# Two layers of segmented memory attention and ReLU feed-forward: part of the first segment's elementwise work goes from VectorE to GpSimd

## The chip, the cores and the metric

The kernel runs on one core of a Trainium2 chip. The time is device microseconds of one execution. Five engines work side by side: TensorE (PE in the profile, PEld for its weight loads), VectorE (DVE), ScalarE (ACT), GpSimd (POOL) and SyncE (SP), which here only issues DMAs. Each engine has its own queue and takes its instructions strictly in order; they wait for each other through semaphores.

## What is computed

The input x has 2048 tokens of 640 features. Two layers follow each other with the same weights; each adds attention and then a feed-forward block to x, both on a layer-normalised x. Attention has 32 heads of 20 features and works in 4 segments of 512 tokens: causal softmax attention inside the segment, mixed by a gate per head with a read from a memory of the earlier segments.

```
phi = lambda t: jnp.where(t > 0, t + 1.0, jnp.exp(t))
g = _sigmoid(beta).reshape(1, H, 1, 1)
for s in range(N):
    qs, ks, vs = (q[:, :, s].copy(), k[:, :, s].copy(), v[:, :, s].copy())
    logits = jnp.einsum('bhqd,bhkd->bhqk', qs, ks) * scale + mask
    a_dot = jnp.einsum('bhqk,bhkd->bhqd', _softmax(logits, axis=-1), vs)
    pq = phi(qs)
    a_mem = num / den                    # pq @ M, pq @ z
    o = g * a_mem + (1.0 - g) * a_dot
    pk = phi(ks)
    M = M + jnp.einsum('bhld,bhle->bhde', pk, vs)
    z = z + jnp.einsum('bhld->bhd', pk)
x = x + o @ wo                           # then x = x + relu(ln(x) @ w1) @ w2
```

The kernel computes phi as min(exp(t), max(t, 0) + 1), which is the same function.

## The kernel before

Everything stays on the chip except the weights' and inputs' loading, a scratch copy of q and k in device memory, and the output.

**Order of the work.** Each engine's order is made when the program is built. Some thirty generators (scores, exps, causal, apply, divide, phi_, mem_write, ffn and so on) each yield one operation at a time: an engine or a choice of two, a planned duration, and what it waits for. A planner (Sched, L224) takes among the heads of all generators the one with the earliest planned start. Added to that start is an offset from the table SHIFT (L175), keyed by generator, phase and how far in the phase it is. A change of any planned duration or engine can give another order on every queue. `pool(600.0, ...)` is an operation of GpSimd planned at 600 ns; the numbers only steer the order.

**One segment of attention.** Normalised tokens (L831, or L843 for the first four tiles) are turned by DMA (L807), or by TensorE for the first four tiles (L856). TensorE projects q and k (L764 for whole weights, L767 for weights loaded in four quarters of 32 columns) and v; VectorE or ScalarE copies the result out of PSUM (L971 and L972 for q and k into stg, L1026 for v). q and k go to device memory and come back as pad, four heads on 32 partitions each (L1060, L1109; the first heads directly, L1089). Two groups of four heads make one step m of 10 half rounds: TensorE makes two halves at a time (one score round, L1293), ScalarE takes the exponential of each half (L1357, 128x1024), GpSimd zeroes what lies above the diagonal (L1369: 1, 2, 2, 1 and 2 selects in the five rounds of a step). TensorE then multiplies the probabilities by v (L1389; two groups of the first segment by tokens, L1428). The result is copied out (L1399, otu), turned by DMA (otk, L807), and divided by its row sum times 1 - g: a reciprocal (L1475), a product with omg (L1478), and two products of 128x320 (L1483, o_sb). The first segment has four steps: 40 exponentials, 32 selects, 20 score rounds; three of its steps go through L1483.

**Memory.** phi of the keys (L1136 max and add, L1138 exponential in place, L1139 min) is turned by DMA (phk), multiplied with v (L1230), copied to M_sb (L1245) and multiplied by maskg (L1257), which keeps each head's own block and carries the gate g. maskg is made once, in consts(): GpSimd fills it with ones (L711) and cuts the blocks out with ten selects (L716, L719); VectorE multiplies each of its five parts by g (L727). g and 1 - g come from L703 to L707. Later segments read the memory (L1172, L1184 to L1187) and add it (L1502).

**Afterwards** o_sb is turned (L807, oT), projected (L764 or L767 with wo_r), added to x (L1511), normalised (L785, L787, L797, rstd by a power on GpSimd, L801), and fed to the feed-forward block, whose last addition is L1606; results are stored by L1638 and L1634. Projections of later segments fill the time in which TensorE would wait for the exponentials of earlier ones.

The two helpers that choose the engine:

```
def dve(n, mode, fn, waits=(), extra=0.0, acq=None, urgent=False, port=False):
    op = Op([("dve", 66.0 + n / (0.96 * mode) + extra, [(fn, True)], 95.0)], waits, ...)
def pool(ns, fn, waits=()):
    return Op([("pool", ns, [(fn, True)], 60.0)], waits)
```

Of the kernel before, what the change touches and what calls it, by code (L numbers as in the profile page):

```python
# [12 lines left out]
DH = 20  # L13
# [146 lines left out]
class Spawn:  # L160
# [15 lines left out]
    (0, 0, 0): -12, (0, 1, 1): -26, (0, 2, 0): -50, (0, 3, 0): -50, (1, 0, 0): -312, (1, 0, 1): -1663,  # L176
    (1, 0, 2): -925, (1, 1, 0): 400, (1, 1, 2): -475, (1, 2, 0): 300, (1, 2, 2): 887, (1, 3, 1): 100, (1, 3, 2): 125,
    (1, 4, 2): 1000, (1, 5, 0): 700, (1, 5, 1): 675, (1, 5, 2): 700, (1, 6, 0): 575, (1, 6, 1): -500, (1, 6, 2): -288,
    (1, 7, 0): 100, (1, 7, 2): 300, (2, 0, 0): -100, (2, 0, 1): -663, (2, 0, 2): -1075, (2, 1, 0): 400,
    (2, 1, 1): -100, (2, 1, 2): -1175, (2, 2, 0): -275, (2, 2, 1): -275, (2, 2, 2): -275, (2, 3, 0): 2387,  # L180
    (2, 3, 2): 1125, (2, 4, 0): -700, (2, 4, 1): -7250, (2, 4, 2): 1951, (2, 5, 1): 388, (2, 5, 2): 725,
    (2, 6, 0): 2000, (2, 6, 1): 2237, (2, 6, 2): 2325, (2, 7, 0): -5250, (2, 7, 1): 2000, (2, 7, 2): 2000,
    (3, 0, 0): -288, (3, 0, 2): -575, (3, 2, 1): -188, (3, 3, 0): -75, (3, 3, 1): -50, (3, 5, 0): -50, (3, 6, 0): -50,
    (3, 6, 1): -250, (3, 7, 1): -350, (5, 0, 0): -5225, (5, 1, 0): 500, (5, 3, 0): -1988, (5, 5, 0): -100,
    (5, 6, 0): 50, (5, 7, 0): -3000, (6, 1, 1): -100, (6, 2, 0): 38, (6, 2, 1): 425, (6, 3, 0): 50, (6, 3, 1): -50,
    (6, 5, 0): 100, (6, 6, 1): -375, (7, 0, 0): -1500, (7, 1, 0): -1525, (7, 2, 0): -300, (7, 3, 0): 200,
    (7, 4, 0): -300, (7, 7, 0): -1500, (8, 2, 0): -774, (8, 2, 1): -75, (8, 2, 2): -6000, (8, 3, 1): -50,
    (8, 4, 0): -175, (8, 4, 1): -100, (8, 6, 0): -50, (8, 7, 0): 3000, (8, 7, 1): 3500, (8, 7, 2): 3000,
    (9, 0, 0): -25, (9, 0, 1): -88, (9, 0, 2): -100, (9, 2, 2): -1725, (9, 3, 0): -225, (9, 3, 1): -87,
    (9, 3, 2): -225, (9, 4, 1): -50, (9, 4, 2): -200, (9, 5, 0): -325, (9, 5, 1): -1388, (9, 5, 2): -200,  # L190
    (9, 6, 0): -400, (9, 6, 1): -287, (9, 6, 2): -1500, (9, 7, 0): 1000, (9, 7, 1): 1000, (9, 7, 2): 1000,
    (10, 0, 0): -100, (10, 0, 1): -37, (10, 1, 0): -1100, (10, 1, 1): -725, (10, 3, 0): 700, (10, 4, 1): -1500,
    (10, 5, 0): -100, (10, 5, 1): -600, (10, 6, 0): -1500, (10, 6, 1): 500, (10, 7, 1): -375, (11, 0, 0): -38,
    (11, 0, 1): -1276, (11, 1, 0): -1550, (11, 1, 1): -650, (11, 2, 0): -50, (11, 2, 1): -225, (11, 3, 0): -1075,
    (11, 3, 1): -3125, (11, 4, 1): 400, (11, 5, 1): -300, (11, 6, 0): -1000, (11, 6, 1): -50, (11, 7, 0): 700,
    (12, 0, 2): -225, (12, 1, 0): 2274, (12, 1, 1): 2274, (12, 2, 0): 5175, (12, 2, 1): -3537, (12, 3, 0): 125,
    (12, 3, 1): -700, (12, 4, 0): 3000, (12, 4, 1): 3000, (12, 5, 0): -375, (12, 5, 1): -200, (12, 6, 0): 4500,
    (12, 7, 0): 1500, (12, 7, 1): 4750, (13, 0, 0): -888, (13, 1, 0): 200, (13, 2, 0): 7413, (13, 3, 0): -50,
    (13, 4, 0): 300, (13, 5, 0): 2113, (13, 7, 0): 1100, (14, 1, 0): -225, (14, 2, 0): -300, (14, 3, 0): -1575,
    (14, 5, 0): -200, (14, 6, 0): -1000, (14, 7, 0): 7863, (15, 0, 0): -238, (15, 0, 1): -62, (15, 2, 0): -350,  # L200
    (15, 2, 1): -300, (15, 4, 1): 412, (15, 5, 0): 425, (15, 6, 1): -450, (16, 2, 1): 75, (16, 3, 0): 638,
    (16, 3, 1): -112, (16, 5, 0): 237, (16, 5, 1): 188, (16, 6, 0): 100, (16, 6, 1): 100, (16, 7, 0): -575,
    (16, 7, 1): -150, (17, 1, 0): 25, (17, 3, 0): -337, (17, 6, 1): -487, (17, 7, 1): 12, (18, 1, 1): -275,
    (18, 2, 1): -75, (18, 3, 0): -50, (18, 3, 1): -100, (18, 5, 1): 200, (19, 0, 0): 500, (19, 2, 0): 500,
    (19, 4, 0): 25, (19, 5, 0): -3850, (20, 1, 0): 138, (20, 1, 1): -75, (20, 2, 0): -200, (20, 2, 1): 50,
    (20, 4, 0): 63, (20, 4, 1): 225, (20, 5, 1): 25, (20, 6, 0): 50, (20, 6, 1): -700, (21, 0, 0): -1788,
    (21, 0, 1): 100, (22, 0, 0): 100, (23, 0, 0): -100, (26, 0, 0): 500, (27, 1, 0): -88, (27, 1, 1): -75,
    (27, 3, 1): 62, (27, 5, 0): 500, (27, 5, 1): 137, (27, 7, 0): 300, (27, 7, 1): 50, (28, 0, 0): 475,
# [287 lines left out]
def pool(ns, fn, waits=()):  # L496
    return Op([("pool", ns, [(fn, True)], 60.0)], waits)
# [8 lines left out]
def bass_interleave_layers__memory_aug_infini_attn__dense_activation_relu__prompt_kernel(  # L506
    nc, A_x, A_wq, A_wk, A_wv, A_wo, A_beta, B_x, B_w1, B_w2, out,
):
    with contextlib.ExitStack() as es:
# [169 lines left out]
        def consts():  # L679
# [6 lines left out]
                pattern=[[-1, 128]], channel_multiplier=1), [t0])  # L686
            S.set("ident", tks=[t1])
            th = yield pool(100, lambda e: e.memset(mhalf[:], -0.5))
            S.set("mhalf", tks=[th])
            yield Need("xt", 0, 0, 1)  # L690
            tv = []
            for b in range(2):
# [1044 lines left out]
```

## Time and profile before

| what | value |
|---|---|
| runs | 550.38, 552.99, 553.38 us; median 552.99 |
| the profiled execution | 550.77 us, of which span 548.3 us |
| TensorE clock granted | full in all of the span |
| first matmul's start, last matmul's end | 1.15 us, 545.4 us |
| first score round, 20th score round | 17.97 us, 58.21 us |
| first exponential, end of the 40th | 18.40 us, 60.58 us |
| busy 18 to 60 us, of 42: PE, DVE, ACT, POOL | 39.7, 39.6, 40.2, 26.7 us |
| busy 70 to 500 us, of 430: PE, DVE, ACT, POOL | 430.0, 352.0, 341.5, 160.5 us |
| DMA engines busy 18 to 36, 36 to 60, 70 to 500 us | 94%, 93%, 50% |

A row of the timeline has the start, the time from the first start to the last end of the merged instructions, engine, line, operation, out<-in, shape and count, and in brackets the idle time before it with what ended it. Neighbouring instructions of one engine overlap by about 0.08 us, so that a busy time is somewhat more than the pace. A busy TensorE is not TensorE at its pace, since the ends of matmuls are modelled; starts are measured.

### The profile page before, as it was taken

Reading aid. Unit: us, or ns where it says so; the run is one execution under the profiler, and the core shown is the slowest. Engines: PE = TensorE matmul, PEld = TensorE weight load, DVE = VectorE, ACT = ScalarE, POOL = GpSimd, SP = SyncE. Lnnn points to the kernel's source line nnn. Section 1 sums busy time; section 2 is a strip of 40 time slices with the busy share of each in tenths; the row PEclk is TensorE's granted clock in tenths of the full one; section 3 lists DMA queues with packets and bytes.
Section 4 is the critical chain, followed back from the end, with each engine's and each line's share of the span. In section 5 each row is a group of like instructions: output and inputs, shape, how many; then the busy total and the mean of one; then the engine's idle time right before and its main releaser. Section 6 shows DMA issues by size and latency. Waiting matters only on the chain.

```text
span 548.3 us, 22987 instructions
## 1 busy us (share of the span) xinstructions
PE 540.1 (99%) x10283; PEld 309.9 (57%) x10283; DVE 424.7 (77%) x1060; ACT 409.9 (75%) x522; POOL 196.8 (36%) x305
## 2 busy tenths in 40 slices
PE   8999999999999999999999999999999999999997
PEld 7434465455554555545465554665456655657766
DVE  4999898798889789987798887989688877637102
ACT  6899979899878898788888878886787776551140
POOL 2655533343444334343344444334333322301000
PEclk9999999999999999999999999999999999999999
DMA  8799789845635326375384614571265611340401
GB/s 272 189 231 259 162 179 203 222 86 105 164 83 89 78 39 163 78 114 77 115 144 114 110 31 140 115 126 26 52 179 102 122 34 28 80 83 15 88 4 51
DMA packets 133476, 62.36 MB, mean 114 GB/s; under 512 B 112258, under 2 KB 123266, under 8 KB 133378
## 3 DMA queue, kind: packets, MB, share of 16 engines
q1 hardware_dynamic: 132832, 60.38, 50.8%
q8 instruction: 81, 1.33, 1.0%
q10 hardware_dynamic: 546, 0.52, 0.3%
q14 instruction: 17, 0.14, 0.1%
HBM read 20.57 MB, written 12.85 MB: 61 GB/s over the span
## 4 chain that ended last, share of the span: by engine, by line
PE 89%; DVE 4%; DMA 4%; POOL 1%; ACT 1%; SPq 1%; issue 1%
PE ps L767 48%; PE ps L764 22%; PE ps L1293 9%; PE ps L1389 6%; PE ps L1172 2%; DMA scr<-stg 1%; DMA x_sb<-in_A_x_dram 1%; PE ps L1230 1%; DMA otk<-otu 1%; PE ps L1564 1%; ACT PT L1357 1%; DVE stats L785 1%; POOL PT L1369 1%; SPq L615 0%; POOL rstd L801 0%
## 5 line engine op out<-in xcount | busy, mean ns | idle before, releaser
L1357 ACT ACTIVATE PT<-ps 128x1024 bf16<-128x1024 f32 x320 | 309.3, 1023 | 61.6 <-PE ps L1293 57.6
L1369 POOL TENSOR_SCALAR_AFFINE_SELECT PT<-PT 128x512 bf16<-128x512 bf16 x256 | 169.9, 681 | 247.6 <-ACT PT L1357 247.6
L767 PE MATMUL ps<-xnT,w_r 128*32 128x512 bf16 x1856 | 110.9, 379 | 0.0
L767 PE MATMUL ps<-w_r,hT 128*32 128x320 bf16 (+1 forms) x1876 | 72.7, 295 | 0.0
L767 PEld LDWEIGHTS ps<-xnT,w_r 128*32 128x32 bf16 x1856 | 46.7, 97 | 44.6 <-issue 5.0
L1293 PE MATMUL ps<-pad 20*128 20x512 bf16 (+3 forms) x1024 | 63.3, 301 | 0.0
L764 PE MATMUL ps<-w_r,hT 128*128 128x320 bf16 x376 | 60.3, 300 | 0.0
L1606 DVE TENSOR_TENSOR x_sb<-x_sb,ps 128x320 bf16<-128x320 bf16 (+1 forms) x65 | 30.7, 475 | 37.8 <-PE ps L767 35.6
L785 DVE BATCH_NORM_STATS2 stats<-x_sb 128x6 f32<-128x320 bf16 x124 | 55.2, 474 | 3.9 <-DMA x_sb<-in_A_x_dram 3.3
L767 PEld LDWEIGHTS ps<-w_r,hT 128*32 128x32 bf16 x1876 | 47.9, 97 | 12.4 <-issue 1.6
L1293 PEld LDWEIGHTS ps<-pad 20*128 20x128 bf16 x1024 | 17.8, 92 | 51.1 <-issue 25.0
L764 PEld LDWEIGHTS ps<-w_r,hT 128*128 128x128 bf16 x376 | 34.7, 98 | 17.5 <-issue 5.0
L1587 ACT ACTIVATE hT<-ps 128x512 bf16<-128x512 f32 x52 | 31.1, 598 | 17.9 <-PE ps L767 17.3
L1586 DVE TENSOR_SCALAR hT<-ps 128x512 bf16<-128x512 f32 x52 | 35.3, 680 | 11.7 <-PE ps L767 9.0
L1511 DVE TENSOR_TENSOR x_sb<-x_sb,ps 128x320 bf16<-128x320 bf16 x64 | 30.1, 478 | 15.5 <-PE ps L767 12.1
L801 POOL TENSOR_TENSOR rstd<-lnU,mhalf 128x2 f32<-128x2 f32 (+2 forms) x27 | 21.0, 778 | 56.2 <-DVE lnU L797 42.8
L1389 PE MATMUL ps<-PT,v_aug 128*21 128x128 bf16 (+3 forms) x896 | 40.3, 300 | 0.0
L1399 DVE CAST otu<-ps 128x512 bf16<-128x512 f32 x50 | 34.1, 683 | 7.9 <-PE ps L1389 7.6
L971 DVE CAST stg<-ps 128x512 bf16<-128x512 f32 x42 | 28.5, 683 | 8.4 <-PE ps L767 7.1
L1483 DVE TENSOR_TENSOR o_sb<-otk,rden 128x320 bf16<-128x320 bf16 x62 | 33.9, 571 | 0.6
L831 DVE TENSOR_SCALAR xn_tok<-x_sb,mv,rstd 128x640 bf16<-128x640 bf16 x60 | 29.8, 519 | 3.4 <-POOL rstd L801 3.4
L1138 ACT ACTIVATE stg<-stg 128x512 bf16<-128x512 bf16 x50 | 31.6, 631 | 0.4 <-DVE rtmp L1136 0.4
(113 smaller groups left out, 706.7 us busy)
## 6 DMA issues: line engine op xcount, KB each, us to landing
pad<-scr SPq DMA_DIRECT2D x124, 80.0 KB
scr<-stg SPq DMA_DIRECT2D x34, 256.0 KB, 2.6
out_dram<-x_sb SPq DMA_DIRECT2D x15, 160.0 KB, 2.2
w_r<-in_B_w_dram SPq DMA_DIRECT2D x10, 216.0 KB, 3.8
w_r<-in_B_w_dram SPq DMA_DIRECT2D x13, 160.0 KB, 2.9
x_sb<-in_A_x_dram SPq DMA_DIRECT2D x10, 160.0 KB, 3.3
scr<-w_r SPq DMA_DIRECT2D x5, 256.0 KB, 4.0
wv_r<-in_A_wv_dram SPq DMA_DIRECT2D x1, 800.0 KB, 7.7
```

What stands on the lines that cost most here:

```text
L764: return e.matmul(view(dst.ap, b), a, b, start=(k == 0), stop=(k == last))
L767: return e.matmul(view(dst.ap[rows], b), part, b, start=(k == 0), stop=(k == last))
L785: tk = yield dve(320, 1, lambda e, c2=c2: e.bn_stats(stats6[:, t, c2, :], x_sb[:, t, c2 * 320:(c2 + 1) * 320]), xt)
L1138: te = yield act(512, lambda e, q=q: e.activation(q, q, ACT.Exp), [tr] + p, psum=False)
L1293: fns.append([(lambda e, z=z, j=j, hh=hh, N=N, o=o, sl=sl, q=hh % 2: e.matmul(slot.ap[:, q, o:o + N], sl.ap[32 * hh:32 * hh + DH, z, 0, 12 ...
L1357: tx = yield act(1024, lambda e, dst=dst, src=src: e.activation(dst, src, ACT.Exp, scale=SCALE), sc + pw)
L1369: tm = yield pool(600.0, lambda e, reg=reg: e.affine_select(out=reg, in_=reg, pattern=[[0, 4], [1, 128]], compare_op=ALU.is_ge, fill=0.0, ...
L1389: fns.append((lambda e, OD, j=j, hh=hh: e.matmul(OD.ap[32 * hh:32 * hh + DH + 1, 128 * j:L], VAUG[vx(a, s)][:, j, 4 * g + hh, :], pt.ap[:, ...
L1399: te = yield evac(L, 1, lambda e: e.tensor_copy(dst, OD.ap), lambda e: e.activation(dst, OD.ap, ACT.Copy), [tk] + OTU[0].tks)
L1483: to = yield dve(320, 1, lambda e, z=z, dst=dst: e.tensor_tensor(dst, av[:, z, :, :, 0:DH], rd.ap[:, z].to_broadcast([128, NJ, 4, DH]), AL ...
L1586: th = yield evac(512, 1, lambda e: e.tensor_scalar(hT[:, dc, :], bk.ap[:, :], 0.0, None, ALU.max), lambda e: e.activation(hT[:, dc, :], b ...
L1587: lambda e: e.activation(hT[:, dc, :], bk.ap[:, :], ACT.Relu), [tk] + HT.tks)
```

## The change

1. consts(): the masks' memset and ten selects stand ahead of the constants that VectorE fills and ahead of the gate; they still wait for the fourth normalised tile.
2. consts(): the five products of masks and gate go from VectorE to GpSimd.
3. phi_: max(k, 0) + 1 of the first segment's keys in the first layer (five instructions) goes from VectorE to GpSimd.
4. divide: in the first segment of the first layer the two products of each of the three turned steps (q < 3, six instructions) go from VectorE to GpSimd.
5. SHIFT has other offsets throughout, so every engine's queue has another order. The number of score rounds, exponentials and DMAs stays; more projections use whole weights and fewer use quarters (9515 matmuls instead of 10283).

```
 SHIFT = {
-    (0, 0, 0): -12, (0, 1, 1): -26, (0, 2, 0): -50, (0, 3, 0): -50, (1, 0, 0): -312, (1, 0, 1): -1663,
...
+    (0, 2, 0): -100, (0, 2, 1): -100, (0, 3, 0): -25, (0, 6, 1): -12, (0, 7, 0): -12, (1, 0, 0): 12, (1, 1, 0): -575,
...
@@ consts
             S.set("mhalf", tks=[th])
+            ntk = yield Need("normed", 3)
+            t3 = yield pool(700, lambda e: e.memset(maskg[:], 1.0), ntk)
+            tmm = []
+            for c in range(FC):
...
+                tmm.append(tm)
             yield Need("xt", 0, 0, 1)
...
             S.set("omg", tks=[to])
-            ntk = yield Need("normed", 3)
-            t3 = yield pool(700, lambda e: e.memset(maskg[:], 1.0), ntk)
-            tmm = []
-            for c in range(FC):
...
-                tmm.append(tm)
             tms = []
...
-                tm = yield dve(140, 1, lambda e, mc=mc, h0=h0, h1=h1: e.tensor_tensor(
-                    mc, mc, gt[:, 2, h0:h1][:, :, None].to_broadcast([128, h1 - h0, DH]), ALU.mult), [tg] + tmm, port=True)
+                tm = yield pool(500, lambda e, mc=mc, h0=h0, h1=h1: e.tensor_tensor(
+                    mc, mc, gt[:, 2, h0:h1][:, :, None].to_broadcast([128, h1 - h0, DH]), ALU.mult), [tg] + tmm)
@@ phi_
-                    tr = yield dve(512, 4, lambda e, rt=rt, q=q: e.tensor_scalar(
-                        rt.ap, q, 0.0, 1.0, ALU.max, ALU.add), p + rt.tks)
+                    lift = lambda e, rt=rt, q=q: e.tensor_scalar(rt.ap, q, 0.0, 1.0, ALU.max, ALU.add)
+                    tr = yield (pool(650.0, lift, p + rt.tks) if a == 0 and s < 1 else dve(512, 4, lift, p + rt.tks))
@@ divide
-                to = yield dve(320, 1, lambda e, z=z, dst=dst: e.tensor_tensor(
-                    dst, av[:, z, :, :, 0:DH], rd.ap[:, z].to_broadcast([128, NJ, 4, DH]), ALU.mult), [tg] + OSB[0].tks, port=True)
+                scale = lambda e, z=z, dst=dst: e.tensor_tensor(
+                    dst, av[:, z, :, :, 0:DH], rd.ap[:, z].to_broadcast([128, NJ, 4, DH]), ALU.mult)
+                to = yield (pool(600.0, scale, [tg] + OSB[0].tks) if (a, s) == (0, 0) and q < 3 else
+                            dve(320, 1, scale, [tg] + OSB[0].tks, port=True))
```

## The prediction

> **What bounds the kernel now.** I read the page's busy line and its chain first, then one table of busy time by stretch, then the timelines of TensorE, ScalarE and GpSimd over the first 65 us.
>
> ```profile
> PE 540.1 (99%) x10283; PEld 309.9 (57%) x10283; DVE 424.7 (77%) x1060; ACT 409.9 (75%) x522; POOL 196.8 (36%) x305
> ...
> PE 89%; DVE 4%; DMA 4%; POOL 1%; ACT 1%; SPq 1%; issue 1%
> ```
>
> TensorE is busy all the time and holds 89% of the chain. A busy row can hide waiting, so I measured pace: for each kind of matmul (shape, and kind of the next one) the median time from its start to the next start, for example 0.216 us for 128x512 and 0.136 for 128x320. Summed over all 10,283 matmuls in their order this gives 535.1 us; from the first matmul's start (1.15) to the last one's it took 544.1. So 8.9 us is waiting: 1.9 in 5 to 10 us, 0.45 in 10 to 20, none in 20 to 30, 1.3 in 30 to 40, 1.7 in 40 to 50, 0.7 in 50 to 60, 0.35 in 60 to 70, and 2.5 as crumbs over the last 480 us (one gap there is over 0.06). After 70 us there is nothing to win; a change of the other engines can win only what lies before.
>
> ```profile
> 18.00:36.00 18.00, 16.98 (x176) 7.66 (x176) 17.06 (x43) 16.32 (x21) 12.69 (x23) 1.00 0.94 226
> 36.00:60.00 24.00, 22.67 (x351) 10.18 (x350) 22.52 (x52) 23.86 (x26) 14.04 (x22) 1.00 0.93 242
> ...
> 70.00:500.00 430.00, 430.00 (x8269) 242.63 (x8272) 352.00 (x876) 341.51 (x423) 160.48 (x239) 1.00 0.50 104
> ```
>
> The columns are stretch, PE, PEld, DVE, ACT, POOL, granted clock, DMA share. From 18 to 60 us VectorE (39.6 of 42) and ScalarE (40.2 of 42) are both nearly full, GpSimd is not (26.7).
>
> ```profile
> 15.04 0.84 PE L764 MATMUL ps<-wv_r,xnT 128*128 128x320 bf16 x5 [0.21 <-DMA wv_r<-in_A_wv_dram]
> ...
> 33.12 0.72 PE L1389 MATMUL ps<-PT,w_r 128*21 128x512 bf16 x16 [0.38 <-DVE w_r L971]
> 34.49 1.05 PE L767 MATMUL ps<-hT,wk_r 128*32 128x512 bf16 x16 [0.64 <-DVE w_r L971]
> ```
>
> The two waits at 33 us are VectorE's: it copies PSUM late, behind a queue without a gap. This is what the change works on. But the next view limits what it is worth:
>
> ```profile
> 26.37 1.94 ACT L1357 ACTIVATE PT<-ps 128x1024 bf16<-128x1024 f32 x2 [0.30 <-PE ps L1293]
> 28.53 0.63 ACT L1138 ACTIVATE stg<-stg 128x512 bf16<-128x512 bf16 x1 [0.23 <-DVE rtmp L1136]
> 29.21 5.61 ACT L1357 ACTIVATE PT<-ps 128x1024 bf16<-128x1024 f32 x6
> 35.90 24.68 ACT L1357 ACTIVATE PT<-ps 128x1024 bf16<-128x1024 f32 x26 [1.08 <-PE ps L1293]
> ```
>
> From 35.90 to 60.58 ScalarE does 26 exponentials of scores without a gap, (24.68 - 1.04) / 25 = 0.946 us each. A score round on TensorE feeds two, so rounds can come every 1.89 us. The 8th round starts at 35.47 and the 20th, the segment's last, at 58.21: 1.895 apart. At TensorE's own pace they would be 20.3 / 12 = 1.69 apart. So the waits of 36 to 58 us are not VectorE's but ScalarE's; only who is named as last differs.
>
> **The change, part by part.**
>
> *The masks' memset and ten selects* (0.7 + 4.4 us of GpSimd, now at 18.97 to 27.93) go ahead of the second segment's rstd, into GpSimd's idle 8.85 to 18.01. 5.1 us fit in 9.2, so they cost nothing; with the cover gone rstd at 18.0 and the two turns behind it would be late. It frees 5 us of GpSimd where the new work goes.
>
> *Sixteen instructions leave VectorE.* Rows, 17 to 64 us:
>
> ```profile
> L1483 DVE TENSOR_TENSOR o_sb<-otk,rden 128x320 bf16<-128x320 bf16 x6 | 3.6, 608 | 0.0
> ...
> L1136 DVE TENSOR_SCALAR rtmp<-stg 128x512 bf16<-128x512 bf16 x5 | 2.0, 405 | 0.5 <-DMA scr<-stg 0.5
> L727 DVE TENSOR_TENSOR maskg<-maskg,gt 128x140 bf16<-128x140 bf16 x4 | 2.0, 488 | 0.0
> ```
>
> With the fifth L727 (0.3) that is 7.9 us, and 0.5 in which VectorE stood behind L1136's DMA. In the changed order VectorE's work from the second segment's lnU to the segment's first by-token reciprocal, priced by start-to-start times (512 wide copies 0.60, 320 wide casts and statistics 0.40, min 0.34, normalising 0.40), is 31.7 us in some 40. VectorE has room; the waits at 33 us and the 0.59 before 41.79 go.
>
> *The same sixteen on GpSimd.* No row shows them there. The nearest:
>
> ```profile
> L1369 POOL TENSOR_SCALAR_AFFINE_SELECT PT<-PT 128x512 bf16<-128x512 bf16 x256 | 169.9, 681 | 247.6 <-ACT PT L1357 247.6
> L801 POOL TENSOR_TENSOR rstd<-lnU,mhalf 128x2 f32<-128x2 f32 x16 | 11.7, 732 | 41.3 <-DVE lnU L797 39.3 <-DVE rmem L1184 1.5
> ...
> L719 POOL TENSOR_SCALAR_AFFINE_SELECT maskg<-maskg 128x147 bf16<-128x147 bf16 x4 | 1.5, 376 | 0.3
> ```
>
> Low end: a select of the same width. 0.64 undisturbed at 512 and 0.37 at 147 make 0.26 + 0.74 ns an element: lifts 0.64, masks 0.38, divisions 0.50, together 8.1 us. High end: the smallest two-input row (power, 128x1) takes 0.56; with two operands at the select's pace a division is 0.56 + 0.47 = 1.03 and a mask 0.78, and each of the sixteen stretched by 0.2 (as L716 is, 0.37 to 0.57): 16.5 us. I take 12: the operations are selects' kin, not powers. GpSimd then has 32 selects at 0.61 + 3 rstd at 1.0 + 12 = 34.5 us from 18.0 to the segment's last select near 60.7, so 81%. The changed order puts most of them in rounds that bring one select, where 1.89 - 0.61 = 1.28 us is free; the probabilities' consumers (L1389) stand 0.5 to 1.3 us ahead of the exponential that needs their buffer. So I cost this at nothing; that slack is the cover. The Trainium skill, "GPSIMD Engine Reference", section 3.1, speaks against moving such work: about 2.6 cycles an element at 1.2 GHz for two inputs. By it a division is about 0.95 us (an estimate with my 0.26 added), the sixteen 11.8 us, and the sum stays; no row here shows it.
>
> *Queues moved past.* GpSimd: a division waits for a turned output (otk); one turn took 3.9 us from issue to landing at 35.45, another 4.8 at 45.84, and selects queue behind a waiting division. SP: the second segment's normalised tiles are turned behind pad fills, the first segment's last fills behind the third segment's turns. Before, that last set was issued at 33.5 to 34.6 and read at 50.5, some 16 us of cover. I cost both at nothing.
>
> *The offsets* reorder every queue. TensorE's work stays the same: 160 score rounds, 900 matmuls' worth of 512 columns (more of them whole, fewer in quarters), 535.2 us by the same prices against 535.1. The tail keeps its cover: the last segment's output projection follows the last attention product by 12.6 us of TensorE work (14.5 before), for a chain that took 11.3 before and loses three of the four additions (1.2) standing last in it.
>
> **The sum.** The wait for wv (landed 14.90) stays, so the start wins nothing. The first score round stands three 320 wide matmuls earlier: 17.97 - 0.41 = 17.56 (its pads landed at 16.58), the first exponential at 17.99. Ahead of the 20th round ScalarE owes 37 exponentials (35.0), and in the changed order between them four key exponentials at 0.54, two copies at 0.5 and one of 0.15 (3.3, against 2.5 before): 56.3, and 0.2 to start, 56.5. The round stands at 50.50 us of TensorE work against 50.98 before. Behind pace: 58.21 - 50.98 = 7.2 before, 56.5 - 50.5 = 6.0 after. **Gain 1.2 us.** The 0.35 at 60 to 70 may go too; more cannot.
>
> 550.77 (span 548.3 and 2.4 around it) less 1.2 is 549.6. The runs shown are 550.38, 552.99 and 553.38; with the profiled one their middle is 551.9, and a new median should lie near the middle, so I write 550.7.
>
> **Rivals.**
>
> *VectorE is the bound* (0.10). For it: its full queue, and the names in the waits of 33 to 42 us. Then all 4.1 us from 30 to 70 go: 550.8 - 4.1 = 546.7. Against it: ScalarE's gapless 24.7 us.
>
> *GpSimd becomes the bound, slower* (0.13). Place: selects in the first segment. Room for the sixteen is 42.7 - 19.5 - 3 = 20.2 us, 1.26 each; from there every further us delays the exponentials. At 1.6 each it is 5.4 over: 550.8 - 1.2 + 5.4 = 555.0. For it: the power's 0.56 to 1.0 for at most four elements. Against it: a two-input product is no power.
>
> *The stalls form again* (0.17). While GpSimd runs, VectorE's rows stretch: L1483 0.84 against 0.53, L831 0.74 against 0.43. With GpSimd at 81% instead of 64%, and a division of about 0.8 us in the way, some 15 exposed instructions could lose 0.43 each, 6.5 us of VectorE's 8 spare, or a select waits once behind a division for its turn (1 to 2 us). The gain is eaten: 550.8 to 551.8 on the profiled run's scale. The Trainium skill, "SBUF — State Buffer", section "Who interferes with whom", says that such a VectorE instruction and GpSimd exclude each other for the whole instruction; the stretched rows agree.
>
> **Chances.** Forecast 0.60, rivals 0.10, 0.13, 0.17. Half a per cent, 2.8 us, is about what a measurement of this kernel can tell from no change. Faster by more: the first rival and a little of the forecast's scatter, 0.13. Slower by more: the second and a little of the third, 0.15. Within: 0.72. The range runs from the lowest run shown less the largest gain I allow (550.4 - 1.6, rounded down for scatter) to 554.5, just under the GpSimd case at 555.0; it leaves out the first rival and most of the second.
>
> **What would show it.** Right: exponentials without a gap from the first to the 40th, VectorE with idle time between 30 and 58 us, the 20th score round near 56.5, GpSimd's new rows at 0.4 to 1.1 us, no wait over 0.1 us on TensorE after 70 us. Wrong: GpSimd rows over 1.3 us, L1389 waiting for L1371's selects, or new waits in the body, which the offsets could make anywhere.

## The result, and the profile after

The changed kernel takes 553.76 us (median of 20 runs, 552.29 to 556.36) against 551.56 us of the kernel before (20 runs, 549.45 to 553.38): a ratio of 1.0045, 95% interval 1.0033 to 1.0056. It is slower by 2.2 to 2.5 us. The forecast was 550.7 us and no change that can be told. The profiled execution has a span, from its first instruction to its last, of 551.2 us against 548.3. The time has a part outside the span, 2.4 us (median) in the kernel before and 1.8 in the changed one; what sets that part is not shown. Inside the span the loss is therefore larger, 2.9 us in these two profiles.

The busy row and the chain of the page of the changed kernel stand beside those of before:

```profile
PE 541.2 (98%) x9515; PEld 306.0 (56%) x9515; DVE 420.9 (76%) x1039; ACT 412.0 (75%) x527; POOL 209.6 (38%) x321
...
PE 86%; DVE 5%; DMA 3%; POOL 3%; SPq 1%; ACT 1%; issue 0%
```

GpSimd is busy for 12.8 us more (16.6 us of new instructions, while its old ones take less: the selects alone 2.8 us less), and TensorE's share of the chain went from 89% to 86%. By the pace count of the prediction (the median start-to-start time of each kind of matmul, with the same prices), TensorE's work is the same, 535.18 us against 535.11. What changed is waiting: 12.31 us against 8.94, +3.37. The tail behind the last matmul is 0.53 us shorter and the first matmul 0.05 us earlier, and 3.37 + 0.07 - 0.53 - 0.05 is the 2.86 us by which the span grew.

The waiting did not grow where the change works. Up to 70 us it is 6.50 us (6.45 before). After 70 us it is 5.79 us (2.47 before). The busy times by stretch of the changed kernel (columns as in the prediction: stretch, PE, PEld, DVE, ACT, POOL, clock, DMA share):

```profile
18.00:36.00 18.00, 16.82 (x168) 8.11 (x167) 16.73 (x45) 16.59 (x22) 14.94 (x16) 1.00 1.01 212
36.00:60.00 24.00, 22.83 (x313) 9.61 (x311) 18.76 (x41) 23.45 (x26) 20.02 (x32) 1.00 1.05 240
70.00:500.00 430.00, 427.74 (x7458) 238.09 (x7459) 349.44 (x861) 345.87 (x432) 159.27 (x240) 1.00 0.51 103
```

VectorE was relieved as planned, 35.5 us of the 42 from 18 to 60 us in place of 39.6, and GpSimd is at 35.0. The third row is new: TensorE, which was busy for 430.0 of 430 us, now is for 427.7. What it waited for there, as the table of waits after 70 us shows it for the changed kernel (waited for, us in total, times, longest):

```profile
PE ps L1295 <- DMA pad<-scr: 0.8, 1, 0.8
PE ps L769 <- issue: 0.6, 1, 0.6
PE ps L769 <- DMA xnT<-xn_tok: 0.5, 1, 0.5
PE ps L1174 <- DVE phs L1141: 0.3, 1, 0.3
```

The same table of the kernel before has no row at all. Three of the four waits are for transfers; the one put down to "issue" also stands at a matmul that reads a turned tile (xnT), which landed at 182.24 us, 0.1 us before the matmul. None of the four is a wait for one of the sixteen moved instructions, which are over at 64 us.

In the first segment the new rows of GpSimd are these, with the select for comparison:

```profile
L1371 POOL TENSOR_SCALAR_AFFINE_SELECT PT<-PT 128x512 bf16<-128x512 bf16 x256 | 167.1, 671 | 251.7 <-ACT PT L1359 251.7
...
L1138 POOL TENSOR_SCALAR rtmp<-stg 128x512 bf16<-128x512 bf16 x5 | 9.9, 1977 | 0.6 <-DMA pad<-stg 0.6
...
L1485 POOL TENSOR_TENSOR o_sb<-otk,rden 128x320 bf16<-128x320 bf16 x6 | 4.5, 749 | 1.0 <-DVE rden L1480 0.9
...
L729 POOL TENSOR_TENSOR maskg<-maskg,gt 128x140 bf16<-128x140 bf16 x4 | 1.7, 439 | 0.0
```

Divisions (0.75 us) and mask products (0.44 us) lie between the forecast's low and high end. A lift (max and add, L1138) takes 1.98 us, three times a select of the same shape. ScalarE's timeline in the changed kernel shows what that does: the exponential of the keys (L1140) waits for its lift.

```profile
20.81 0.63 ACT L1140 ACTIVATE stg<-stg 128x512 bf16<-128x512 bf16 x1 [0.37 <-POOL rtmp L1138]
...
29.71 0.63 ACT L1140 ACTIVATE stg<-stg 128x512 bf16<-128x512 bf16 x1 [0.89 <-POOL rtmp L1138]
30.25 14.78 ACT L1359 ACTIVATE PT<-ps 128x1024 bf16<-128x1024 f32 x16
45.58 14.86 ACT L1359 ACTIVATE PT<-ps 128x1024 bf16<-128x1024 f32 x16 [0.55 <-PE ps L1295]
```

So the theory to test had two parts: **the new order of the queues makes the waits after 70 us**, and **the lifts eat the gain of the first segment**. Rivals: the later waits are the late first segment handed on (A), the lifts do not hold the first segment (B), GpSimd and VectorE slow each other (C), VectorE is the first segment's bound (D), the selects come late behind the new instructions (E).

### The profile page after: what moved, and what is told of

Its sections match the earlier page's. It is cut to its first block, busy times and chain, and to the rows that moved or that the text cites. A ratio compares the mean times of both kernels' runs of the same rounds, so it can differ in the third digit from the quotient of the medians.

```text
span 551.2 us, 21460 instructions
## 1 busy us (share of the span) xinstructions
PE 541.2 (98%) x9515; PEld 306.0 (56%) x9515; DVE 420.9 (76%) x1039; ACT 412.0 (75%) x527; POOL 209.6 (38%) x321
## 4 chain that ended last, share of the span: by engine, by line
PE 86%; DVE 5%; DMA 3%; POOL 3%; SPq 1%; ACT 1%; issue 0%
PE ps L769 39%; PE ps L766 30%; PE ps L1295 8%; PE ps L1391 6%; DVE stats L787 2%; PE ps L1174 2%; DMA x_sb<-in_A_x_dram 1%; POOL PT L1371 1%; POOL rtmp L1138 1%; PE ps L1232 1%; DMA xnT<-xn_tok 1%; PE ps L1568 1%; DVE stg L973 1%; DMA pad<-scr 1%; DMA pad<-stg 0%; DVE phs L1141 0%
## 5 line engine op out<-in xcount | busy, mean ns | idle before, releaser
L769 PE MATMUL ps<-xnT,w_r 128*32 128x512 bf16 x1380 | 84.3, 379 | 0.0
L769 PE MATMUL ps<-w_r,hT 128*32 128x320 bf16 (+1 forms) x1772 | 68.7, 295 | 0.0
L766 PE MATMUL ps<-w_r,hT 128*128 128x320 bf16 x402 | 65.0, 300 | 0.0
L1591 ACT ACTIVATE hT<-ps 128x512 bf16<-128x512 f32 x60 | 35.7, 599 | 34.4 <-PE ps L769 30.9
L769 PEld LDWEIGHTS ps<-w_r,hT 128*32 128x32 bf16 x1772 | 44.0, 97 | 13.2 <-issue 1.6
L769 PEld LDWEIGHTS ps<-xnT,w_r 128*32 128x32 bf16 x1380 | 33.9, 97 | 30.7 <-issue 2.9
L973 DVE CAST stg<-ps 128x512 bf16<-128x512 f32 (+2 forms) x55 | 36.6, 666 | 8.5 <-PE ps L769 4.8
L766 PE MATMUL ps<-xnT,w_r 128*128 128x512 bf16 x175 | 41.8, 380 | 0.0
L1391 PE MATMUL ps<-PT,v_aug 128*21 128x128 bf16 (+3 forms) x896 | 40.3, 300 | 0.0
L803 POOL TENSOR_TENSOR rstd<-lnU,mhalf 128x2 f32<-128x2 f32 (+2 forms) x27 | 21.2, 785 | 39.6 <-DVE lnU L799 38.5
L1590 DVE TENSOR_SCALAR hT<-ps 128x512 bf16<-128x512 f32 x44 | 30.0, 682 | 6.3 <-PE ps L766 3.0
L1140 ACT ACTIVATE stg<-stg 128x512 bf16<-128x512 bf16 x50 | 31.5, 632 | 2.5 <-POOL rtmp L1138 1.3
L769 PE MATMUL ps<-wo_r,oT 128*32 128x320 bf16 x788 | 31.9, 300 | 0.0
```

Of the source, the lines that this page charges most:

```text
L766: return e.matmul(view(dst.ap, b), a, b, start=(k == 0), stop=(k == last))
L769: return e.matmul(view(dst.ap[rows], b), part, b, start=(k == 0), stop=(k == last))
L973: te = yield evac(N, 1, lambda e: e.tensor_copy(sg.ap[:, t0:t0 + N], bk.ap[:, 0:N]), lambda e: e.activation(sg.ap[:, t0:t0 + N], bk.ap[:, ...
L1140: te = yield act(512, lambda e, q=q: e.activation(q, q, ACT.Exp), [tr] + p, psum=False)
L1391: fns.append((lambda e, OD, j=j, hh=hh: e.matmul(OD.ap[32 * hh:32 * hh + DH + 1, 128 * j:L], VAUG[vx(a, s)][:, j, 4 * g + hh, :], pt.ap[:, ...
L1591: lambda e: e.activation(hT[:, dc, :], bk.ap[:, :], ACT.Relu), [tk] + HT.tks)
```

## The experiments

Two tools were built into the planner. One lets a picked instruction be planned on one engine and issued on another, so that the order of all the rest stays word for word:

```diff
-            self.P.waits(e, waits)
+            ee = op.emit or e; self.P.waits(ee, waits)
...
-                    tk = self.P.op(e, fn, mark)
+                    tk = self.P.op(ee, fn, mark)
```

The other lets the planner follow, from a given planned time of TensorE, the recorded order of picks of another kernel (the earliest in that list of those that are ready, with the engine and the matmul form recorded there):

```diff
-            _, st, end, start, k, op = best
+            best = self.follow(heads) if redo else best; _, st, end, start, k, op = best
```

with `redo = self.free['pe'] > 66000`, for example. All runs in one table. "Waits" are TensorE's by the pace count, in the profiled execution. "40 exponentials" is the time on ScalarE from the start of the first exponential of scores to the end of the 40th, the first segment's last. In e7, e12 and e14 the granted clock was at half for some time, and the count holds what TensorE lost by that as well: 1.7, 10.8 and 10.3 us (half of its busy time in those stretches).

| run | median us (before) | ratio, 95% interval | waits to 70 us | waits after | 40 exponentials |
|---|---|---|---|---|---|
| before | 551.56 | | 6.45 | 2.47 | 42.18 |
| changed | 553.76 (551.56) | 1.0045, 1.0033 to 1.0056 | 6.50 | 5.79 | 42.46 |
| e1 | 552.93 (550.56) | 1.0046, 1.0029 to 1.0063 | 6.47 | 4.90 | 41.59 |
| e2 | 554.50 (550.56) | 1.0066, 1.0047 to 1.0086 | 7.56 | 5.74 | 43.10 |
| e3 | 554.08 (550.56) | 1.0066, 1.0048 to 1.0084 | 8.08 | 5.53 | 41.81 |
| e4 | 554.99 (550.56) | 1.0075, 1.0055 to 1.0094 | 7.29 | 6.79 | 42.53 |
| e5 | 551.65 (550.76) | 1.0021, 1.0005 to 1.0037 | 7.11 | 3.38 | 41.59 |
| e6 | 552.50 (550.76) | 1.0032, 1.0016 to 1.0047 | 7.02 | 4.68 | 42.15 |
| e7 | 555.95 (550.76) | 1.0096, 1.0071 to 1.0121 | 12.11 | 2.84 | 48.07 |
| e8 | 552.68 (550.76) | 1.0048, 1.0028 to 1.0068 | 7.06 | 4.91 | 42.47 |
| e9 | 553.59 (551.22) | 1.0039, 1.0025 to 1.0054 | 8.22 | 4.89 | 42.51 |
| e10 | 551.86 (551.22) | 1.0008, 0.9995 to 1.0021 | 6.62 | 4.90 | 42.28 |
| e11 | 550.48 (551.22) | 0.9991, 0.9972 to 1.0009 | 6.98 | 2.48 | 41.49 |
| e12 | 595.81 (551.22) | 1.0814, 1.0789 to 1.0840 | 8.07 | 44.4 | 41.50 |
| e13 | 552.99 (550.87) | 1.0033, 1.0020 to 1.0045 | 6.78 | 5.40 | 42.66 |
| e14 | 598.50 (550.87) | 1.0869, 1.0847 to 1.0890 | 10.91 | 43.9 | 45.94 |

The part of the time outside the span is 2.44 us (median) in the kernel before, and 1.75 in e9, e10 and e11. So the spans compare otherwise than the times. Their medians lie above that of the kernel before in the same series by 2.6 us in e1, 4.3 in e2, 1.2 in e5, 2.5 in e6, 3.05 in e9, 1.4 in e10 and 0.05 in e11.

### The order or the late first segment: e2, e3, e4, e9

**e2: the order alone.** All sixteen instructions issued on VectorE, nothing else moved:

```diff
-                    tr = yield (pool(650.0, lift, p + rt.tks) if a == 0 and s < 1 else dve(512, 4, lift, p + rt.tks))
+                    tr = yield (on("dve", pool(650.0, lift, p + rt.tks)) if a == 0 and s < 1 else dve(512, 4, lift, p + rt.tks))
```

and the same for the mask products and the divisions.

> The changed kernel's plan and order kept, with all sixteen instructions (lifts, mask products, divisions) put back on VectorE, so that what is left of the change is the order that the new offsets make, and the masks built early. Theory: TensorE waits after 70 us stay within 0.5 us of the changed kernel's 6.0 us, the first 70 us come back to 5.5 to 6.5 us; time 553 to 554.3, ratio 1.003 to 1.005. Rival A (late first segment handed on): about 550.5 to 551.5, ratio 0.998 to 1.000. Rival C (GpSimd and VectorE slow each other): about 551.5, ratio 1.000.

The waits after 70 us are 5.74 us, the changed kernel's 5.79, though not one of the instructions is on GpSimd any more. The table of TensorE's waits after 70 us of e2:

```profile
PE ps L1232 <- DMA phk<-phs: 0.8, 1, 0.8
PE ps L769 <- issue: 0.7, 1, 0.7
PE ps L1174 <- DVE phs L1141: 0.3, 1, 0.3
PE ps L1295 <- DMA pad<-scr: 0.3, 1, 0.3
```

Three of the places are the changed kernel's; the fourth shows that a transfer's landing scatters from one execution to the next. The time, 1.0066, is higher than the theory gave (1.003 to 1.005), and in its profile the first segment with everything on VectorE is 0.6 us slower than the changed kernel's, not equal to it. Rival C, by which 551.5 us were due once GpSimd had no new work, falls as well.

**e3 and e4: halves exchanged.** e3 is the changed kernel up to about 71 us and then the order of before; e4 the other way.

> The changed kernel up to 66 us of planned TensorE time (all sixteen instructions on GpSimd, as in the change), and from there every pick in the order that the kernel before makes. Theory: no TensorE wait over 0.3 us after 75 us, waits after 70 us back to about 2.7 us, the first 70 us stay at 6.5 us; time 551.6, ratio 0.9985 to 1.0015. Rival A (late first segment handed on): the waits after 70 us stay, 553.5 and more, ratio over 1.003.

> The kernel before up to 66 us of planned TensorE time (all sixteen on VectorE, masks late), and from there every pick in the order that the changed kernel makes. Theory: the waits near 82, 92, 136, 181 and 378 us come back, about 3.3 us in all; time 554.8, ratio 1.004 to 1.007. Rival A (late first segment handed on): none of them, 551.6, ratio 1.000.

Where the two orders meet, both kernels pay a seam that neither theory foresaw: 2.62 us of waits at 70 to 80 us in e3, 1.11 in e4. So their times say little: e3 missed its 551.6 us (554.08), and e4 met its 554.8 (554.99) with 1.1 us of seam in it. The waits from 80 us on do tell. In e3 they are 2.91 us, although its start is the changed kernel's with the slow lifts; in e4 they are 5.68, although its start is the old one. TensorE's waits from 80 us on, e3 and then e4:

```profile
PE ps L1295 <- ACT PT L1359: 0.6, 1, 0.6
PE ps L769 <- DMA xnT<-xn_tok: 0.4, 1, 0.4
```

```profile
PE ps L767 <- DMA xnT<-xn_tok: 0.8, 1, 0.8
PE ps L767 <- DMA oT<-o_sb: 0.6, 1, 0.6
PE ps L764 <- DMA xnT<-xn_tok: 0.4, 1, 0.4
PE ps L764 <- issue: 0.2, 1, 0.2
```

(The 0.6 of e3 ends at 80 us and is still the seam's.) Of the five places named ahead for e4, waits came back near 136 and 378 us, hardly near 92 us (0.1) and not near 82 and 181; the others of e4 stand elsewhere (91, 249 and 498 us). So it is the sum of the waits that goes with the order of the body and not with the start, more than the places: rival A falls.

**e9: the changed kernel once more**, with no edit.

> The changed kernel once more, to stand beside the others on the same chip. All theories: ratio 1.003 to 1.0055; TensorE waits after 70 us 5 to 6.5 us; the five lifts 1.98 us each.

1.0039, with 4.89 us after 70 us. Six profiles now have the changed kernel's order after 70 us (changed, e1, e2, e8, e9, e13): 5.79, 4.90, 5.74, 4.91, 4.89, 5.40, mean 5.27. Three have the old one (before, e7, e11): 2.47, 2.84, 2.48, mean 2.60. **The order costs 2.7 us**, nearly all of the 3 us by which the span grew (2.9 in the first two profiles, 3.05 in the medians of e9's series).

### The lifts: e1, e7, e8

**e1: the lifts back on VectorE**, by the diff shown at e2 and nothing more.

> The changed kernel with the planner's choices, offsets and every queue's order kept, and only the five lifts put back on VectorE. Theory (the loss has two parts: the new order makes 3.3 us of waits after 70 us, and in the first 70 us the lifts, 1.98 us each on GpSimd, eat a gain of about 1.2 us): the waits of ScalarE for the lift buffer (0.37 and 0.89 us) go, the first 70 us lose about 1 us of TensorE waits (6.5 to about 5.5), the waits after 70 us stay near 3.3 us above before's; time 552.8, ratio to before 1.002 to 1.0035. Rival A (the waits after 70 us are the late first segment handed on): they go too, time about 549.5, ratio 0.996. Rival B (the first segment is not held by the lifts): time 553.8, ratio 1.0045.

ScalarE's waits in the first segment of e1:

```profile
ACT w_r L1028 <- PE ps L766: 2.5, 1, 2.5
ACT PT L1359 <- PE ps L1295: 0.8, 3, 0.4
ACT stg L1140 <- DVE rtmp L1138: 0.2, 1, 0.2
```

The wait for the lift fell from 1.26 us to 0.15, and the 40 exponentials take 41.59 us in place of 42.46 (42.51 in e9). e5, e6 and e9 have the same start and agree: that wait is 0.2 us with the lifts on VectorE (e5), 1.1 and 1.5 with the lifts on GpSimd (e6, e9). The 40 exponentials scatter more, 41.59 twice (e1, e5) against 41.81 to 42.66 in five profiles with this start and the two-operation lifts on GpSimd. So the lifts on GpSimd cost the first segment some 0.7 to 0.9 us, and rival B falls. The first row, 2.5 us, is the value weights, which landed 9.35 us after their issue in this execution (7.64 in the changed one); it hides the gain in the waits to 70 us. In the total the expected 1.002 to 1.0035 was not met: 1.0046, beside 1.0039 of e9, with intervals that overlap widely. 0.9 us is too little for the total to tell.

**e7: the lifts moved alone**, in the order of before.

```diff
-                    tr = yield dve(512, 4, lambda e, rt=rt, q=q: e.tensor_scalar(
-                        rt.ap, q, 0.0, 1.0, ALU.max, ALU.add), p + rt.tks)
+                    tr = yield on("pool" if a == 0 and s < 1 else None, dve(512, 4, lambda e, rt=rt, q=q: e.tensor_scalar(
+                        rt.ap, q, 0.0, 1.0, ALU.max, ALU.add), p + rt.tks))
```

> The kernel before with its planner's choices, offsets and every other queue's order kept, and only the five lifts sent to GpSimd. Theory (a lift there takes about 2 us, and the selects and ScalarE's exponentials wait behind it): ScalarE waits for the lift buffer, TensorE for late selects, 20 to 70 us lose 1 to 2.5 us more than the 4.1 us of before; no new wait over 0.3 us after 80 us; time 551.6 to 553.1, ratio 1.002 to 1.0045. Rival B (the lifts are not what holds): 550.6, ratio 1.000.

1.0096: 5.2 us lost (median of four runs), more than twice the upper end that was expected. The waits after 70 us stay at 2.84. ScalarE's waits, and TensorE's clock by stretch, in e7:

```profile
ACT stg L1138 <- POOL rtmp L1136: 6.3, 4, 2.3
```

```profile
34.00:36.00 2.00, 0.00 (x1) 0.01 (x2) 1.16 (x3) 1.83 (x3) 1.06 (x3) 1.00 0.76 206
...
37.00:38.00 1.00, 1.00 (x4) 0.33 (x3) 1.00 (x4) 1.00 (x2) 1.00 (x3) 0.50 0.81 242
38.00:39.00 1.00, 1.00 (x6) 0.14 (x8) 0.73 (x2) 0.46 (x1) 1.00 (x1) 0.50 0.73 217
39.00:40.00 1.00, 1.00 (x20) 0.29 (x16) 0.91 (x2) 0.64 (x1) 1.00 (x2) 0.50 0.66 162
```

ScalarE, whose exponentials pace the segment, stands four times behind a lift that takes 1.94 us where the plan has 0.2. The waits that this gives TensorE (1.2, 0.8, 1.1 and 2.2 us between 23 and 36 us) bring a second loss in the profiled execution: its granted clock is half for 3.41 us, some 1.7 us more. (The four executions list a mean clock of 0.997, 0.997, 1.0 and 1.0, so two of them went without it.) The Trainium skill, "TensorE: Matmul & The Clock Gate", section "What's actually happening", puts the gate at half the clock after an idle window of about 3.4 us, which need not start with the wait; the half clock agrees; an idle window of that length does not show here, where no single wait was longer than 2.2 us.

**e8: a lift of one operation.**

```diff
                     lift = lambda e, rt=rt, q=q: e.tensor_scalar(rt.ap, q, 0.0, 1.0, ALU.max, ALU.add)
-                    tr = yield (pool(650.0, lift, p + rt.tks) if a == 0 and s < 1 else dve(512, 4, lift, p + rt.tks))
+                    tr = yield (pool(650.0, lambda e, rt=rt, q=q: e.tensor_scalar(rt.ap, q, 1.0, None, ALU.max), p + rt.tks)
+                                if a == 0 and s < 1 else dve(512, 4, lift, p + rt.tks))
```

> The changed kernel with its order kept, each lift on GpSimd as one operation, max(k,1), in place of two, max(k,0)+1; it leaves out the addition, so phi is another function in the first segment's keys of the first stream. If the price of a lift goes by the number of operations it halves, to about 1.0 us, and then by the theory most of ScalarE's 1.26 us of waits for the lift buffer and the 0.9 us select wait near 43 us go: 20 to 70 us lose 3.3 us in place of 4.1, while the waits after 70 us stay; time 553.0, ratio 1.003. If the price goes by the elements it stays at 1.98 us, and nothing else changes: 553.8, ratio 1.0045. If it were slowed by VectorE beside it, its five durations would scatter by more than 0.1 us.

```profile
L1139 POOL TENSOR_SCALAR rtmp<-stg 128x512 bf16<-128x512 bf16 x5 | 9.0, 1790 | 0.9 <-DMA pad<-stg 0.6 <-DMA scr<-stg 0.2
```

Neither price came: 1.79 us on the mean, 9% less for half the operations, and the time stayed (1.0048). But the five are 1.70, 2.51, 1.49, 1.65 and 1.61 us: they scatter by 1.0 us, which was the sign named for a slowing by VectorE, while the five of the changed kernel lie between 1.92 and 2.08. Without the second one the mean is 1.61, 19% less. So one operation fewer saves less than half; what stretched the second lift was not tried, and neither was a lift of fewer elements. In the changed kernel two lifts in a row take 3.92 us and the next instruction starts 1.94 us after the second one's start, so there the 1.98 us is the pace at which the engine gets through them, and not a record that is too long.

### What is left when the lifts stay and the old order returns: e5, e6, e10, e11

**e5 and e6.** The changed order up to 88 us of planned time, where the plans differ by 8 instructions only, then the old order; e5 with the lifts on VectorE, e6 with them on GpSimd.

> The changed kernel's order up to 88 us of planned TensorE time (some 94 us in the profile), with the lifts put back on VectorE and the mask products and divisions left on GpSimd; from there every pick in the order of the kernel before. At 88 us the two plans have issued the same work but for 8 instructions. Theory (the order makes the loss after 70 us, the lifts eat the gain before): the waits near 82 and 92 us stay, those near 136, 181, 237 and 378 us go; waits after 95 us come to about 2.1 us, from the changed kernel's 4.0; with the lifts back that is 2.8 us less than the changed kernel, time 551.0, ratio 0.998 to 1.001. Rival A (late first segment handed on): the waits after 95 us stay as long as the divisions are on GpSimd; ratio 1.003 to 1.005. Rival B (lifts do not hold the first segment): 551.8, ratio 1.001 to 1.002.

> As the run before, with the lifts left on GpSimd (all sixteen as in the change). Theory: 20 to 70 us as in the changed kernel (about 4.1 us of TensorE waits), about 2.1 us of waits after 95 us, time 551.9, ratio 1.000 to 1.002. Rival A: the waits after 95 us stay at 4 us, ratio 1.0045.

1.0021 and 1.0032: both lower than the changed kernel's 1.0045, in the expected order, and both 0.1% above the upper end of what was expected. The two differ by the lifts alone, on one chip and in eleven runs each: 0.85 us of time, 1.3 us of span. The seam is not free: a memory read at 152 us waits 0.59 us in both profiles, which it does not in either parent, and in e6 another 0.8 us are lost at 351 us. From 100 us on the waits are 3.07 and 3.89 us, not 2.1.

**e10: three parts.** With lifts on VectorE, mask products and divisions on GpSimd: the old order to 13 us of planned time, the new one to 88 us, then the old.

> The kernel before up to 13 us of planned TensorE time, then the order of the changed kernel up to 88 us, then the order of the kernel before; lifts on VectorE, mask products and the first segment's divisions on GpSimd. Theory, with a third part that the runs so far suggest (the changed kernels' starts lose 0.9 us more than the old ones, by a late landing of the value weights: 1.25 against 0.46 us of that wait): 0 to 20 us lose 2.2 to 2.7 us, 20 to 70 us 3.3 us, 70 to 95 us 0.3 to 1 us, after 95 us 2.1 to 2.9 us; in all 8.0 to 8.9 us against 8.9 of before; ratio 0.998 to 1.0005. Rival (the start is chance): the start costs as in the run with lifts on VectorE and the old body, ratio 1.002. Rival B (lifts do not hold the first segment): 20 to 70 us lose 4.1 us, ratio 1.001.

1.0008, with 11.5 us of waits where 8.0 to 8.9 were expected: the span is 1.4 us longer than that of the kernel before, while 0.7 us less stand outside it. The wait for the pads of the round at 84.14 us is 1.2 us here, the longest at this round in any profile. The expectation's third part, that the changed kernels' starts lose 0.9 us by a late landing of the value weights, is withdrawn: e11, with the old start, waited 1.86 us at the same place. The wait goes with the landing of that load, 7.6 to 9.35 us after its issue, and it was long and short with either start; whether a small part of it belongs to the start is open.

**e11: mask products and divisions moved alone**, in the order of before (the diff of e7 for L727 and L1483).

> The kernel before with every queue's order kept; only the five mask products and the six first divisions are sent to GpSimd, no lift. By the prediction's reading (ScalarE's exponentials hold the first segment, VectorE has room) taking 4 us of work off VectorE brings nothing: 20 to 70 us lose 4.1 us as before, less at most 0.5; ratio 0.999 to 1.001. Rival D (VectorE is the bound of the first segment): a gain of 1.5 to 4 us, ratio 0.993 to 0.997. Rival E (GpSimd's selects come late behind the new instructions): 20 to 70 us lose 1 us more, ratio 1.002.

0.9991, interval 0.9972 to 1.0009: no change that can be told. The 40 exponentials take 41.49 us in place of 42.18, and the waits of 20 to 70 us 3.38 in place of 4.11. So taking 4 us of work off VectorE brings 0.7 us in this profile, a little more than the 0.5 allowed, and far from rival D's 1.5 to 4. The runs as a whole do not show it: the median span is 548.75 us against 548.70, and the 0.7 us of time lie outside the span. GpSimd's selects do not come late (rival E). In the new order the moves weigh more: the 40 exponentials take 43.10 us with all sixteen on VectorE (e2), 41.59 with the lifts alone there (e1) and 42.46 with none. By these single profiles eleven of the moves are worth 1.5 us there and five cost 0.9; the medians of e2 and e1, 1.6 us apart in time and 1.7 in span, bear out the first. That is the low end of rival D, so in the new order VectorE does hold the first segment in part. e11 is the best version found, and not one that can be told from the kernel before.

### The table of offsets, and one place: e12, e14, e13

**e12 and e14: tables exchanged.** e12 is the changed code with the old table, e14 the old code with the new one.

```diff
 SHIFT = {
-    (0, 2, 0): -100, (0, 2, 1): -100, (0, 3, 0): -25, (0, 6, 1): -12, (0, 7, 0): -12, (1, 0, 0): 12, (1, 1, 0): -575,
...
+    (0, 0, 0): -12, (0, 1, 1): -26, (0, 2, 0): -50, (0, 3, 0): -50, (1, 0, 0): -312, (1, 0, 1): -1663,
...
```

> The changed kernel's code with the old table of offsets: the sixteen instructions on GpSimd, masks early, and the planner left to make an order from offsets that were made for another plan. Theory (the order of the whole body hangs on the table and on every price together, so each moved instruction reorders all of it): waits after 70 us over 5 us, of before's 2.5, in other places than the changed kernel's; ratio 1.004 to 1.012. Rival F (the new table itself is worse than the old one, and the old one would keep the body): waits after 70 us about 2.5 us, ratio 0.999 to 1.002.

> The kernel before with the changed kernel's table of offsets and nothing else. If a table fits one plan only, this loses as the moves with the old table did (which cost 8%): several us at least, ratio 1.01 to 1.10, with waits of over 1 us all over the body. If the new table is as good as the old for any plan: ratio 0.998 to 1.005.

8.1% and 8.7% slower, 45 and 48 us: far above what was expected of e12 (1.004 to 1.012), and within what was expected of e14. Not all of it is waiting. The mean granted clock is 0.971 and 0.974: after waits it fell to half in three or four stretches of each profile, which cost TensorE the 10.8 and 10.3 us named above. In e12 the waits pile up at the end, 28.7 us of them after 500 us, some 9 of them by the clock (TensorE's waits there):

```profile
PE ps L1568 <- DMA xnT<-xn_tok: 11.4, 1, 11.4
PE ps L769 <- DMA oT<-o_sb: 4.9, 1, 4.9
PE ps L1391 <- POOL PT L1371: 2.2, 1, 2.2
```

A table fits one plan. Sixteen moved instructions change every planned time behind them, and with it every choice; the new table brings back 42 of the 45 us, and the 2.7 us are what it leaves.

**e13: two instructions exchanged.** In the changed kernel's order a pad fill of the second segment (82.89 us, the sixth of those that go out from 79.11 us on) goes ahead of the turn that it stood behind (81.07 us).

```diff
-L1111 DMACopy pad<-scr 20x2x1024 x5
-L809 DmaTransposeAnt xnT<-xn_tok 128x10x128
-L1111 DMACopy pad<-scr 20x2x1024
+L1111 DMACopy pad<-scr 20x2x1024 x6
+L809 DmaTransposeAnt xnT<-xn_tok 128x10x128
```

> The changed kernel with two instructions exchanged on SyncE's queue and nothing else: the second segment's sixth pad fill goes ahead of the turn of a normalised tile that it stood behind (issued 82.89 and 81.07 us in the changed kernel's profile). Theory (the place in the queue makes the wait): the fill is issued 1.6 to 1.8 us earlier and the score round near 82 us no longer waits (0.19 to 0.89 us in the five profiles with this order); the turn lands some 0.5 us later and no new wait over 0.2 us comes; the waits near 92, 136 and 181 us stay; time 0.6 us less, 553.1, which the total can't tell from no change. Rival (the fill itself, or the buffer that it fills, is late): the wait stays within 0.3 us of what it was.

The fill was issued at 80.88 us, 2.0 us earlier, and the score round waits as before (TensorE's timeline, changed kernel and then e13):

```profile
83.64 0.40 PE L1295 MATMUL ps<-pad 20*128 20x512 bf16 x4 [0.82 <-DMA pad<-scr]
```

```profile
83.96 0.40 PE L1295 MATMUL ps<-pad 20*128 20x512 bf16 x4 [0.87 <-DMA pad<-scr]
```

This does not speak against the theory, since the exchanged fill is not one that this round reads. Four fills make the pad of one step. By the semaphores in the trace the round waits for the four fills issued at 79.11 to 80.31 us, whose last part landed at 83.59 us (83.91 in e13); the fifth and the sixth belong to the next step. And these four do stand late in SyncE's queue (its timeline in the changed kernel, and the row of the same fills in the kernel before):

```profile
60.78 1.71 SPq L1062 DMA_DIRECT2D scr<-w_r  x3
...
70.71 3.00 SPq L809 DMA_TRANSPOSE phk<-phs  x1
...
77.95 1.12 SPq L1062 DMA_DIRECT2D scr<-stg  x1
79.11 1.92 SPq L1111 DMA_DIRECT2D pad<-scr  x5
```

```profile
57.41 3.48 SPq L1109 DMA_DIRECT2D pad<-scr  x9
```

The store that the four fills read last (the first of the three scr<-w_r) landed at 63.16 us, and their buffer's last reader, the tenth score round, ran at 38.89 us. Yet they go out 16 us after that landing, behind seven turns, one of which waits 2.8 us for VectorE, and behind the third segment's five stores (scr<-stg). In the old order the same four go out at 59.04 to 60.17 us, with the third segment's stores far behind them, and have landed 12 us ahead of their round at 75.78; in the changed kernel 0.05 us ahead. So the place in SyncE's queue makes this wait, as far as the traces show; no run moved these four fills, and the other places were not traced back like this.

## Why the prediction was wrong, and where it was right

- **The step that failed: "The offsets reorder every queue", costed at nothing because TensorE's work stays the same and "the tail keeps its cover".** The tail did keep it (the time behind the last matmul's start fell from 3.12 to 2.59 us). But I had looked only at the work and at the tail, and not at what hides the transfers in between. The step next to it costed SyncE's queue at nothing ("Queues moved past") by the cover of one set of fills, the first segment's last; the set that came late is the second segment's, whose cover fell from 12 us to nothing. In the old order no wait after 70 us was over 0.06 us but one; in the new order there are four or five of 0.2 to 1.0 us in each execution, 2.7 us together with the crumbs. The prediction named this among its reasons to fail ("new waits in the body, which the offsets could make anywhere") and gave it neither a price nor a chance. As a rival that ends slower it would have needed a share of its own. That the time still lies below the upper end of the range, 554.5 us, is luck: that end was set by another rival.
- **"Gain 1.2 us": it did not come, by a term that was mis-sized.** Waits to 70 us are 6.50 against 6.45. The first exponential came as worked out (17.98 us, forecast 17.99), but the 20th round at 58.07 us, not 56.5. Of the 1.5 us the lifts are some 0.7 to 0.9 (e1, e5): 1.98 us each in place of the 0.64 at the low end and under 1 at the one taken. The rest is that ScalarE still waits 0.8 us for score rounds even with the lifts back: the step counted 37 exponentials without a gap.
- **"I take 12", for the sixteen:** 16.6 us were measured (9.9 + 2.2 + 4.5), 0.1 above the high end. Divisions (0.75 in 0.50 to 1.03) and masks (0.44 in 0.38 to 0.78) lay inside; the select was the wrong neighbour for the lift. The sixteen average 1.04 us, under the 1.26 at which GpSimd was to become the bound, so by the average all was well. But four of the five lifts stand between 18.85 and 29.68 us, 7.9 us of 10.8, ahead of ScalarE's work: the price had to be put where the instructions stand.
- **The Trainium skill, "GPSIMD Engine Reference", section 4.1, calls one-input instructions of GpSimd roughly line rate.** The trace disagrees: 1.98 us for 512 elements, 3.9 ns each, against 0.75 us for 320 elements with two inputs, 2.3 ns each.
- **Right:** the masks' early place was free (9.36 to 14.0 us, in GpSimd's idle time); VectorE got room (35.5 us busy of 42); GpSimd stood at 83% (forecast 81%); ScalarE, more than VectorE, paces the first segment in the old order (e11 against rival D: 0.7 us at most, and not 4). In the new order the same eleven moves are worth some 1.6 us (e2 and e1).
- **Signs named ahead:** three of those for "wrong" came, lifts over 1.3 us, L1391 (L1389 before) waiting 0.84 us for a select at 43.85 us, and the new waits in the body.

## What to carry to other kernels

Where a planner or a tuned table orders the queues, a moved instruction is a new order, and the order has a price of its own: split the change by keeping every queue's order and moving the instruction alone, and price the two apart. An engine with idle time is not a place for any instruction: price it by a row of the same kind of instruction, and at the place where it stands, since an average over the segment hides four slow ones in a row ahead of the engine that sets the pace. Waits of 0.3 to 0.9 us for transfers that a profile of before does not show at all are the first thing to look for after a reordering; to test one, move the very transfer whose semaphore the waiting instruction waits for, which need not be the nearest in the queue.

## What the runs showed of the hardware

- A TENSOR_SCALAR on GpSimd, 128x512 bf16, takes 1.98 us with two operations (1.92 to 2.08) and 1.79 us with one (1.49 to 2.51, one of five over 1.70); an affine select of the same shape 0.67 us on the mean. In these rows the kind of instruction sets the price more than the number of its operations.
- The same load of the value weights (800 KB), issued at 6.4 to 7.8 us, landed 7.6 to 9.35 us later from one execution to the next; TensorE's wait for it ran from 0.3 to 2.1 us and is the largest scatter between profiles.
- After waits of 1.2, 0.8, 1.1 and 2.2 us within 13 us the granted clock fell to 0.50 (e7), and in e12 after waits of 0.4 to 1.7 us in the 8 us before. In the changed kernel's profile, with no wait over 0.91 us, it did not fall; four of its 20 runs list a mean clock of 0.997.
- The half clock came in stretches of one length and its multiples: 3.41 us in e7, 3.41, 10.24, 6.83 and 13.65 us in e12, 13.65, 10.24 and 6.83 us in e14, leaving out those that reach past the end of the program's instructions.
- The part of the time outside the span differs between kernels that are nearly alike: 2.44 us in the kernel before and 1.75 in e11, where only eleven instructions changed their engine (medians). What sets it is not shown.
